# A retention and gated-MLP kernel on one core: a new written-out order of all its jobs, with other filler matmuls and other gates for transfers

## The chip, the cores and the metric

The kernel runs on one core of one Trainium2 chip. The metric is the device time of one execution in microseconds. Before the change it is 209.71 us as the median of three runs (209.13 to 210.56).

The engines of the core are named as in the profile: PE (TensorE, matmuls), PEld (PE's weight loads), DVE (VectorE), ACT (ScalarE), POOL (GpSimd) and SP (SyncE). In this kernel SP issues nearly all transfers, and it issues them in order: a transfer that waits holds every transfer behind it.

## The reference

The input is eight batches of 576 rows with eight heads of 64 columns. The first stage is a retention layer: attention without a softmax, where each score is multiplied by a power of the head's decay. The second is a gated MLP with a spatial gate, which mixes the 576 rows of a batch by the matrix w_sg.

```python
scores = scale * np.matmul(q, k.transpose(0, 1, 3, 2))
gamma = 1.0 - 2.0 ** (-5.0 - np.arange(H, dtype=np.float32))
rel = pos[:, None] - pos[None, :]
Dmat = np.where(rel >= 0, gamma[:, None, None] ** rel[None, :, :], 0.0)
x = np.matmul(scores * Dmat, v)               # heads side by side: 512 columns
...
h = gelu(x @ w_in)                            # 1024 columns
u, v = (h[..., :512], h[..., 512:])
v_n = (v - mean(v)) / np.sqrt(var(v) + 1e-06) * g_ln
v_s = np.einsum('ts,bsd->btd', w_sg, v_n) + b_sg[None, :, None]
out = x + (u * v_s) @ w_out
```

## The kernel before, in words

The eight batches are taken in four pairs. A pair has 1152 rows, or nine tiles of 128. The retention stage cuts the rows of a pair into five blocks (`RB`): four of 256 rows and one of 128 rows, which joins the end of one batch with the start of the next. So there are 20 blocks and 36 tiles. Most of the names below are those of the buffers that the profile shows.

**A block** goes through these jobs. SP loads q, k and v (`a_load`, L324 and L327; one q load may serve two blocks). POOL, and for block 0 also DVE and ACT, cast them to bf16 and multiply q and v by powers of the decay (`a_prep`, L360 and L370). PE transposes q and k (`a_T`, L407, into pp), DVE copies the transposes out (`a_Tev`, L422, qT). PE forms the scores in two halves (`a_S`, L458), DVE masks them (`a_Sev`, L471, ret). PE forms the running state k'v (`a_Z`, L494, zp), DVE adds it up and ACT casts it (`a_Zsum`, L519 and L522; `a_Zev`, L526 and L528, zb). PE forms the output in two jobs (`a_O`, `a_O2`, L540, pp), and ACT copies it out as the transposed x (`a_Oev`, L597, xT).

**A tile** then goes through these. PE forms the half of h that is normalised (`m_V`, L608, hv), ACT takes its gelu (L615, vg), DVE its mean and variance (`m_stats`, L623 and L624). POOL forms the reciprocal root (`m_rs`, L628 to L631, mv), and ACT normalises (`m_norm`, L643, vn). PE also forms the other half (`m_U`, L655, hu), and ACT takes its gelu (L665, uT).

**A batch**, once its five tiles are normalised, goes through the spatial gate: eight jobs of five matmuls against the transposed w_sg (`m_W`, L674, wp), whose results DVE multiplies into uT (L684). These are called the gating matmuls in the text. Then come the output matmuls of each tile (`m_O`, L706, op), which ACT or DVE copies out (L725, ob), and the stores (L730). The last tile, job pair 911 and 914, is done in two halves of 256 columns.

**Once per launch**: w_in in two halves of 1 MB (jobs 3 and 9, L248) with their casts on DVE and ACT (L255, L257), w_sg in three transfers (15 and 16, L269; 17, its last 64 rows, L273) with five casts on ACT (18 to 22, L280), and w_out (job 26, L291). PE transposes w_sg in ten jobs (83, 85 to 101, `build_wT`, L793, wtp), and DVE copies each out (L797, wT). Small vectors go through `to_col` (job 75, L736) and `to_rows` (77 and 79, L758) on PE.

**The order.** There is no scheduler at run time. `Planner.add` gives every job a number, 0 to 916, in the order in which the code makes them. `ORDER` is a string of these numbers, written out in the source, and `Planner.emit` walks through it and issues each job's instructions. So an engine's order is the order of its own jobs in the string; between engines the semaphores decide. Two more kinds of words stand in the string:

```python
x, _, g = x.partition("@")
j = self.fill(x[1:]) if x[0] == "f" else self.jobs[int(x)]
...
if g:
    hold(made[0], last[g])
```

A word such as `13@77` is a gate: the first transfer of job 13 also waits for the last instruction that PE's job 77 made, and through SP's order all transfers behind it wait too. A word such as `f7w128` is a filler on PE: seven fp32 matmuls of 128 columns of zeros into a scratch tile (scr, L225) that nobody reads. Fillers stand in the string in PE's order like any other job. The old string has six fillers and eight gates.

Buffers are rings with a set number of places, which also make a job wait: eight for loads, two for qT, four PSUM banks of the kind d (hv, hu, wp, op, zp, wtp, scr) and two of the kind pp.

The jobs that the text names: 0, 1, 2 are q, k, v of block 0; 6, 7, 8 those of block 1; 13, 12, 14 k, q, v of block 2; 23, 24, 25 and 31, 32 the loads of blocks 3 and 4; 33 to 37 those of blocks 5 and 6. Job 106 is the transposes of block 0, 199 and 201 its scores, 280 and 283 hv of the first two tiles. Job 293 is the state job of block 1, 203 and 205 its scores, 284 the gelu of the second tile, 297 and 298 the output jobs of block 1. Job 328 is the first gating job, 215 and 334 are a score job of block 4 and a gating job.

Of the kernel before, what the change touches and what calls it, by code (L numbers as in the profile page):

```python
# [17 lines left out]
PR = dict(PB0=10000.0, O=4000.0, PB=9900.0, S=2000.0, S2=400.0, Z=1901.0, V=6000.0, V2=900.0, U=1260.0, W=4000.0, WS=19000.0, slack=60.0, pen=500.0)  # L18

ORDER = (  # L20
# [33 lines left out]
)  # L54


# [1031 lines left out]
```

## Time and profile before

| what | value |
|---|---|
| median of three runs | 209.71 us |
| the profiled execution, its own time | 210.52 us |
| its span in the profile | 208.8 us |
| DVE, ACT, POOL busy | 72%, 56%, 57% |
| PE weight loads busy | 66% |
| chain that ended last: PE, DMA, SP's queue, DVE, POOL | 82%, 5%, 3%, 3%, 2% |
| on that chain: gating wp, output op, hv, hu | 19%, 15%, 14%, 14% |
| on that chain: fillers scr | 2% |
| DMA | 48.36 MB, 232 GB/s in the mean |

The profile is of one execution, and times in it count from the start of the span. PE's busy time is made of modelled ends of pipelined matmuls, so a busy PE isn't PE at its peak. A row of the order of time gives the start, the length of the merged row, engine, line, operation, the tile written and the tiles read, and the count; in brackets stands how long the engine was idle before, and who ended that. A row of the chain gives the start, the length and what it was; the chain is followed back from the last instruction, at each step to what released it.

### The profile page before, as it was taken

To read this page: it belongs to the slowest core of one execution; us is meant where nothing else is said; L and a number is where in the kernel's file an instruction comes from. 1 tells how busy PE (TensorE), PEld (TensorE's weight loads), DVE (VectorE), ACT (ScalarE), POOL (GpSimd) and SP (SyncE) were. 2 spreads that over 40 slices of the span, in tenths; PEclk is the share of its full clock that TensorE was granted. 3 is DMA by queue.
4 is the path that set the end of the run, shared out by engine and by line. 5 is a ranking of instruction groups with operands and counts; after the bars stand their busy time and mean duration, and the time that the engine had idled before them with its cause. 6 is when DMAs were issued, how large, how long until landed. Compare 5 with 4: busy or idle time off the path is not lost.

```text
span 208.8 us, 7892 instructions
## 1 busy us (share of the span) xinstructions
PE 196.0 (94%) x3378; PEld 137.4 (66%) x3408; DVE 151.3 (72%) x291; ACT 116.4 (56%) x207; POOL 118.3 (57%) x169
## 2 busy tenths in 40 slices
PE   7778998899999999999999999999999999999992
PEld 6655774676666676667676777576785576476751
DVE  3587567996478598917788978897885788667573
ACT  5209487574776836478852466835635667553300
POOL 8396275987567889681980996844549134022000
PEclk9999999999999999999999999999999999999999
DMA  6999949987997995999699979996986995883825
GB/s 167 290 342 216 314 150 340 293 254 268 263 279 218 303 292 140 290 262 246 178 203 285 333 244 304 164 241 152 298 219 149 175 255 154 201 152 104 239 87 201
DMA packets 85524, 48.36 MB, mean 232 GB/s; under 512 B 36650, under 2 KB 78898, under 8 KB 85490
## 3 DMA queue, kind: packets, MB, share of 16 engines
q1 hardware_dynamic: 85472, 47.87, 88.3%
q8 instruction: 26, 0.43, 0.9%
q14 instruction: 8, 0.07, 0.1%
q10 hardware_dynamic: 18, 0.00, 0.0%
HBM read 32.79 MB, written 9.44 MB: 202 GB/s over the span
## 4 chain that ended last, share of the span: by engine, by line
PE 82%; DMA 5%; SPq 3%; DVE 3%; POOL 2%; issue 2%; DVEq 0%; POOLq 0%
PE wp L674 19%; PE op L706 15%; PE hv L608 14%; PE hu L655 14%; PE pp L540 7%; DMA ld<-in_v_dram 5%; PE pp L458 4%; PE pp L407 3%; SPq L324 3%; PE zp L494 2%; PE scr L225 2%; POOL vb L370 2%; DVE wT L797 1%; PE op L701 1%; PE wtp L793 1%
## 5 line engine op out<-in xcount | busy, mean ns | idle before, releaser
L471 DVE TENSOR_TENSOR ret<-pp,msk 128x1024 bf16<-128x1024 f32 x32 | 38.3, 1213 | 6.8 <-PE pp L458 6.8
L674 PE MATMUL wp<-wT,vn 128*128 128x288 bf16 x256 | 40.5, 286 | 0.0
L370 POOL TENSOR_TENSOR vb<-ld,gpow 128x1024 bf16<-128x1024 f32 (+1 forms) x20 | 34.5, 1731 | 10.0 <-DMA ld<-in_v_dram 7.6
L608 PE MATMUL hv<-w_in,xT 128*128 128x512 bf16 x129 | 35.7, 386 | 2.1 <-DVE wT L797 0.7
L655 PE MATMUL hu<-xT,w_in 128*128 128x256 bf16 (+1 forms) x320 | 36.5, 262 | 0.3 <-DVE w_in L255 0.3
L706 PE MATMUL op<-w_out,uT 128*128 128x512 bf16 (+1 forms) x133 | 34.3, 373 | 0.9 <-issue 0.2
L684 DVE TENSOR_TENSOR uT<-wp,uT 128x288 bf16<-128x288 f32 x64 | 27.1, 449 | 10.4 <-PE wp L674 8.9
L655 PEld LDWEIGHTS <-w_in 128*128 128x128 bf16 x320 | 28.1, 98 | 6.9 <-DVE w_in L255 0.4
L597 ACT ACTIVATE xT<-pp 128x512 bf16<-128x512 f32 (+1 forms) x40 | 20.3, 552 | 21.1 <-PE pp L540 21.1
L643 ACT ACTIVATE vn<-vg,mv 128x512 bf16<-128x512 f32 x32 | 25.4, 808 | 11.5 <-POOL mv L631 11.3
L665 ACT ACTIVATE uT<-hu 128x512 bf16<-128x512 f32 x36 | 21.0, 595 | 19.3 <-PE hu L655 19.2
L674 PEld LDWEIGHTS <-vn 128*128 128x128 bf16 x256 | 24.6, 98 | 8.4
L628 POOL TENSOR_SCALAR mv<-mv 128x2 f32<-128x2 f32 (+1 forms) x20 | 4.5, 224 | 43.7 <-DVE mv L624 37.2
L615 ACT ACTIVATE vg<-hv 128x512 f32<-128x512 f32 x36 | 21.5, 597 | 12.8 <-PE hv L608 11.8
L623 DVE BATCH_NORM_STATS2 bst<-vg 128x6 f32<-128x512 f32 x36 | 24.5, 682 | 5.0 <-ACT vg L615 5.0
L370 POOL TENSOR_TENSOR qb<-ldq,gpow 128x1024 bf16<-128x1024 f32 x14 | 26.5, 1902 | 2.4 <-DMA ldq<-in_q_dram 2.3
L725 DVE TENSOR_TENSOR ob<-op,xr 128x512 f32<-128x512 f32 (+1 forms) x28 | 18.5, 669 | 7.7 <-PE op L706 6.1
L608 PEld LDWEIGHTS <-xT 128*128 128x128 bf16 x144 | 13.4, 99 | 14.7 <-ACT xT L597 1.7
L706 PEld LDWEIGHTS <-uT 128*128 128x128 bf16 x148 | 13.6, 98 | 12.0
L674 PE MATMUL wp<-wT,vmid 128*128 128x288 bf16 x64 | 18.2, 287 | 0.0
L360 POOL CAST kb<-ld 128x1024 bf16<-128x1024 f32 x14 | 14.4, 1038 | 4.6 <-PE pp L540 2.5
L422 DVE COPY qT<-pp 128x2048 bf16<-128x2048 bf16 (+1 forms) x11 | 11.3, 1025 | 6.4 <-PE pp L407 6.4
(100 smaller groups left out, 262.2 us busy)
## 6 DMA issues: line engine op xcount, KB each, us to landing
out_dram<-ob SPq DMA_DIRECT2D x35, 256.0 KB, 2.9
ld<-in_k_dram SPq DMA_DIRECT2D x16, 512.0 KB, 5.7
ld<-in_v_dram SPq DMA_DIRECT2D x16, 512.0 KB, 6.9
ldq<-in_q_dram SPq DMA_DIRECT2D x7, 1024.0 KB, 7.6
xT<-in_moe_w_sg_dram SPq DMA_DIRECT2D x2, 576.0 KB, 5.6
ld<-in_q_dram SPq DMA_DIRECT2D x2, 512.0 KB
xT<-in_moe_w_in_dram SPq DMA_DIRECT2D x1, 1024.0 KB, 8.2
ld<-in_k_dram SPq DMA_DIRECT2D x8, 128.0 KB, 3.0
```

Source lines behind the costliest of these rows:

```text
L370: ve.tensor_tensor(dst, src, g.unsqueeze(len(src.shape) - 1).to_broadcast(list(src.shape)), op=Alu.mult)
L471: ins = nc.vector.tensor_tensor(ret[:].rearrange("p r (k t) -> p (r k) t", k=2), sc[:].rearrange("p r (k t) -> p (r k) t", k=2), (msk2 if ...
L597: nc.scalar.activation(dst, src, Act.Copy)
L608: ins = nc.tensor.matmul(hv[:], xTs[p][:, m, kk, :], w_in[:, kk, F2:], start=(kk == 0), stop=(kk == KK - 1))
L615: unfence(nc.scalar.activation(vgs[i][:], cur.pop(("hv", i))[:], Act.Gelu_apprx_tanh), ("V", i))
L623: nc.vector.bn_stats(bst[:], vgs[i][:])
L643: nc.scalar.activation(vn[:], vg[:], Act.Identity, scale=mv[:, s, 2:3], bias=mv[:, s, 3:4])
L655: ins = nc.tensor.matmul(hu[:, n, :], w_in[:, kk, 128 * c:128 * c + 128], xTs[p][:, m:m + w, kk, :], start=(kk == 0), stop=(kk == KK - 1), ...
L665: unfence(nc.scalar.activation(uTs[p][:, c0:c1, 128 * m:128 * m + 128 * w], cur.pop(("hu", i, half))[:], Act.Gelu_apprx_tanh), ("U", i, half))
L674: ins = nc.tensor.matmul(ps[:], vns[t0 + j][e][:, 128 * c:128 * c + 128], wT[e][j][:, half * HS:(half + 1) * HS], start=(j == 0), stop=(j ...
L684: ins = nc.vector.tensor_tensor(uTs[p][:, c, col:col + HS], cur.pop(("wp", b, c, half))[:], uTs[p][:, c, col:col + HS], op=Alu.mult)
L706: ins = nc.tensor.matmul(op[:], uTs[p][:, c, r], w_out[:, c, cs], start=(p >= XP and c == 0), stop=(c == KK - 1), skip_group_check=True)
```

## The change

`ORDER` is replaced by another string of the same 917 jobs; no other line of the kernel differs. It changes the order of every engine, SP among them.

The fillers: the old ones are f2w64, f1w128, f5w64, f4w192, f7w128, f3w256. The new ones are f2w64, f1w256, f1w64, f7w256, f6w256, f2w192, f1w128, f3w192, f1w64, f1w192. All of the new ones stand before block 1's first output job, as all of the old ones do.

The gates: the old ones are 13@77, 9@297, 33@215, 36@361, 48@151, 55@461, 508@489, 745@798. The new ones are 7@75, 9@298, 33@215, 36@334, 44@219, 349@450, 53@481, 55@491, 583@241, nine in all.

PE's jobs up to the first weight transposes, with `to_col` (75) behind the transposes of block 0 instead of before them:

```
before: f2w64 f1w128 f5w64 75 f4w192 106 199 201 77 271 276 277 79 111 280 205 293 f7w128 203 283 116 f3w256 207 297 298 83 101 85
after:  f2w64 f1w256 f1w64 f7w256 106 75 f6w256 199 77 201 271 f2w192 276 277 111 f1w128 280 203 293 205 283 f3w192 116 f1w64 f1w192 79 207 297 83 99 298 89
```

SP's first transfers:

```
before: 1 0 6 2 7 3 8 13@77 12 17 16 15 14 23 9@297 24 31 25 32 34 33@215 26 36@361 35
after:  17 0 1 2 6 7@75 3 8 13 12 15 16 14 23 9@298 24 31 25 32 26 33@215 36@334 34 35
```

ACT's casts of w_sg, in the old list 22 21 20, then the gelu 284, then 19 18; in the new one 22 is ACT's first job, and 284 18 295 19 20 21 follow one another. On DVE the evacuation of block 3's q (123) stood ahead of the statistics 306 and now stands behind them. At the end DVE emptied the two halves of the last tile as 915 912 and now empties them as 912 915; their stores follow the same order.

The diff, cut to the parts of which the text speaks:

```diff
 ORDER = (
-    '1 0 103 f2w64 6 f1w128 f5w64 2 7 75 f4w192 76 104 3 8 106 107 199 200 201 202 108 105 74 109 73 77 13@77 271 '
-    '273 12 276 17 277 278 5 79 279 111 78 72 272 274 4 112 80 16 280 110 113 114 15 14 81 281 205 293 23 f7w128 206 '
-    '203 283 116 282 294 296 204 117 f3w256 207 275 295 22 21 20 284 19 18 297 9@297 298 82 299 115 285 208 24 83 31 '
-    '101 85 317 318 290 25 32 118 119 84 102 320 300 291 319 292 97 89 86 90 98 91 95 321 87 322 92 96 93 301 304 '
-    '122 94 323 88 302 11 305 10 303 123 306 326 120 124 34 286 309 99 100 314 316 287 310 311 126 121 307 127 315 '
...
-    '893 898 901 894 899 895 908 902 903 909 910 904 905 906 911 914 915 912 916 913 '
+    '17 0 22 f2w64 1 103 72 2 6 104 f1w256 f1w64 105 73 108 f7w256 106 75 107 76 7@75 109 3 f6w256 8 13 199 200 12 '
+    '77 201 202 271 f2w192 273 276 277 110 113 114 78 272 111 f1w128 274 4 112 278 5 15 16 280 279 275 14 203 23 293 '
+    '205 283 204 281 282 294 81 284 18 295 19 20 21 206 296 285 f3w192 116 f1w64 f1w192 79 117 207 208 80 297 83 74 '
+    '290 115 99 84 100 298 9@298 89 90 91 24 95 31 101 102 92 317 25 93 94 96 318 85 86 97 98 314 315 87 32 118 119 '
+    '291 292 320 300 319 299 82 321 322 316 323 326 11 120 124 88 10 304 301 302 122 305 303 306 123 26 286 309 288 '
...
+    '887 891 896 888 897 889 893 898 901 894 899 895 902 903 904 905 906 908 909 910 911 914 912 915 913 916 '
 )
```

54 rows, old and new, of the table ORDER are left out of this document.

## The prediction

> **What bounds the kernel now.** I read the page's busy shares first, then two stretches in the windows view (columns: length, busy time and instructions of PE, PEld, DVE, ACT, POOL, then clock, DMA share, GB/s).
>
> ```profile
> span 208.8 us, 7892 instructions
> PE 196.0 (94%) x3378; PEld 137.4 (66%) x3408; DVE 151.3 (72%) x291; ACT 116.4 (56%) x207; POOL 118.3 (57%) x169
> 0.00:45.00 45.00, 38.22 (x663) 29.30 (x669) 30.96 (x72) 26.11 (x43) 30.67 (x56) 1.00 0.96 258
> 45.00:205.00 160.00, 157.74 (x2721) 108.11 (x2748) 119.61 (x219) 90.29 (x164) 87.68 (x114) 1.00 0.88 225
> ```
>
> From 45 us on PE is busy 157.74 of 160 us. The lists hold the same real PE jobs, so behind 45 us a new order can save at most those 2.3 us. In front of it PE issues a fifth of its instructions in 45 us: the ramp. So I take the chain that ended last, in order of time, up to the first gating matmul (start, length, what):
>
> ```profile
> 8.38 9.96 DMA ld<-in_v_dram
> 18.48 1.91 POOL vb L370
> 20.43 0.64 PE zp L494 x27
> 21.07 3.28 PE scr L225 x14
> 24.35 0.57 PE pp L458 x14
> 24.92 0.42 PE hv L608
> 25.39 0.59 PE hv L608 x2
> 25.99 0.34 PE pp L407 x16
> 26.33 1.49 PE scr L225 x6
> 28.07 0.56 PE pp L540 x40
> 29.06 0.94 PE wtp L793 x15
> ...
> 37.52 1.11 DVE qT L422
> 38.63 0.61 DVE bst L623
> 41.42 1.87 POOL vb L370
> 43.34 0.44 PE zp L494 x32
> 45.63 0.47 PE wp L674 x3
> ```
>
> The chain runs through fillers (scr, L225), matmuls that compute nothing: f7w128 (each fp32 filler is recorded as two matmuls, so x14) for 3.28 us and f3w256 (x6) for 1.49 us, 4.77 us together. They don't fill a wait, they are one: the score job behind f7w128 (203) has the inputs of its twin 205, which stands ahead of the filler in the list. Why so long? PE's order of time:
>
> ```profile
> 1.24 3.67 PE L225 MATMUL scr<-warm 128*128 128x64 f32 x16 [1.24 <-DVE warm L183]
> 6.06 2.93 PE L225 MATMUL scr<-warm 128*128 128x192 f32 x8
> 8.92 1.04 PE L407 MATMUL pp<-ident,qb 64*128 64x64 bf16 x32
> 11.28 1.07 PE L458 MATMUL pp<-qT 64*64 64x128 bf16 x32 [1.32 <-DVE qT L422]
> 16.38 1.04 PE L407 MATMUL pp<-ident,qb 64*128 64x64 bf16 x32
> 17.63 0.59 PE L608 MATMUL hv<-w_in,xT 128*128 128x512 bf16 x1 [0.22 <-DVE w_in L255]
> 56.20 0.64 PE L407 MATMUL pp<-ident,qb 64*128 64x64 bf16 x32
> 60.43 0.42 PE L494 MATMUL zp<-vb,kb 64*64 64x64 bf16 x32
> ```
>
> The same 32 transposes take 1.04 us at 8.92 and 16.38 but 0.64 at 56.20; 27 state matmuls take 0.64 us at 20.43, 32 take 0.42 at 60.43. A filler of 128 columns took 3.28/14 = 0.234 us in the run from 21.07, one of 256 columns 1.49/6 = 0.248 us from 26.33: 1.83 against 0.97 ns a column. PE ran at about half rate until some 25 us, though the clock column says 1.00 throughout. It changed after the one unbroken stretch of work before then, 21.07 to 25.9, 4.9 us. The busy stretch of 6.06 to 9.96, 3.9 us with the transposes, did not change it.
>
> The Trainium skill (TensorE: Matmul & The Clock Gate, Part 1) says that the array starts at half clock and is let go after a busy window of about 3.4 us; the halving agrees, and 4.9 us against 3.9 us fits a window that does not start with the work. By its remark that this ramp costs under 1% of a span, the whole change could give at most 2.1 us; the 3.28 us row alone is larger, so I let the row decide.
>
> **The change, part by part.**
>
> *First fillers.* Before the first transposes (job 106) PE now gets f2w64, f1w256, f1w64, f7w256: 6 matmuls of 64 columns (3.67/16 = 0.23 us) and 16 of 256. At half rate 256 columns are not in the trace: 2.93/8 = 0.366 us for 192 gives 0.49 us, as an estimate. All slow: 1.24 + 1.4 + 7.8 = 10.4 us; with the change of rate after 4.9 us: 7 at 0.49, 9 at 0.25, ending at 8.3. The transposes' inputs were there by 8.92, and come up to 0.5 later now, since 144 KB of w_sg (job 17) are issued ahead of q and k (290 GB/s, row below). So they start at 8.3 to 10.4 instead of 8.92. f6w256 then stands ahead of the first scores: 12 x 0.25 = 3.0 us in a wait of 1.3, so scores at about 12.6 instead of 11.28 (5.9 us and 17.5 if slow: 10.4 + 1.04 + 0.2 + 5.9). Cover: the first hv needs w_in, which ended its wait at 17.63. f2w192, f1w128: under 1.2 us together, in front of the same wait. I count all at nothing; without the cover 1.3 us.
>
> *Fillers on the chain.* Between the state job at 20.43 and the second block's output job stand now f3w192, f1w64, f1w192. Fast: 8 x 0.19 + 2 x 0.19 = 1.9 us; slow: 8 x 0.366 + 2 x 0.23 = 3.4. Against 4.77: -2.9 or -1.4. I take -2.9, because by then PE has had its unbroken 4.9 us twice over.
>
> *Real jobs at full rate.* On the chain zp, 14 scores and hv: 0.64 to 0.42, 0.57 to 0.40, and hv by a quarter of its 1.01: -0.6.
>
> *The gate 7@75.* SP's first five loads are 144 KB and four of 512 KB, 2.2 MB.
>
> ```profile
> 5.00:10.00 5.00, 4.07 (x41) 3.48 (x41) 2.65 (x11) 1.36 (x3) 1.59 (x3) 1.00 1.20 290
> 17.00:19.00 2.00, 1.56 (x19) 0.69 (x14) 2.00 (x3) 1.95 (x4) 0.53 (x1) 1.00 1.00 147
> 27.50:30.20 2.70, 2.58 (x101) 1.97 (x99) 1.75 (x5) 2.17 (x4) 2.37 (x6) 1.00 0.10 35
> 28.68 0.37 SPq L248 DMA_DIRECT2D uT<-in_moe_w_in_dram  x1
> ```
>
> At 290 GB/s they end near 10. Job 7 (block 1's k), behind it w_in's half, v, and all later loads, wait in SP's queue until job 75 has run behind the transposes, 8.8 to 10.6. A gated load's data moves 1.5 us after its issue (28.68, 30.2), so DMA idles 0.3 to 2.1 us. Against that, the old gate 13@77, whose slow stretch is 17 to 19 (147 GB/s), is gone: some 1 us. For v of block 1, the chain's head, -1 to +2.1; I take +0.6.
>
> *The w_sg casts.* They must end before the ten weight transposes (wtp).
>
> ```profile
> 18.12 1.03 SPq L269 DMA_DIRECT2D xT<-in_moe_w_sg_dram  x2
> xT<-in_moe_w_sg_dram SPq DMA_DIRECT2D x2, 576.0 KB, 5.6
> 23.41 1.24 ACT L280 ACTIVATE wnat<-xT 128x576 bf16<-128x576 f32 x2
> 26.08 0.60 ACT L615 ACTIVATE vg<-hv 128x512 f32<-128x512 f32 x1 [1.44 <-PE hv L608]
> 26.58 1.25 ACT L280 ACTIVATE wnat<-xT 128x576 bf16<-128x576 f32 x2
> ```
>
> Two stood behind vg, which waited for the late hv. In the new list vg (284) and all four follow one another, so they end 1.3 us behind the last w_sg data (19.15 + 5.6 = 24.8, an estimate, +0.6): 26.7, against wtp at 29.06: -2.4 there, where the sum above gives -2.9. For wtp the tighter one holds.
>
> *To the first gating matmul.* DVE empties the ten wtp tiles and does the statistics between 29.5 and 39.45. The new list puts the q evacuation (1.11) behind the last of them: -1.1 on DVE, -3.5 with the shift. But POOL's mv job stands behind two k casts, whose loads follow gate 9@298, two wtp later than 9@297 (+0.6): -2.9 + 0.6 = -2.3. POOL, then, sets it: the last vb, the state job and wp come 2.3 us earlier.
>
> *Rest.* Other gates (36@334, 44@219, 349@450, 53@481, 55@491, 583@241) hold SP with loads or stores behind them. Their cover is POOL's spare time: beyond 46 us it waited for q as below and idled mostly for DVE's statistics.
>
> ```profile
> POOL mv L628 <- DVE mv L624: 35.0, 13, 6.2
> POOL qb L370 <- DMA ldq<-in_q_dram: 2.3, 2, 2.0
> ```
>
> The tightest is 36@334, which also holds job 34 (block 5's k): one more 512 KB load, 1.8 us, at the k transposes. I take 0; without cover +1, and by the 2.3 us of PE's idle time the rest may go 1 either way. At the tail DVE empties the halves in PE's order:
>
> ```profile
> 204.98 0.76 DVE L725 TENSOR_TENSOR ob<-op,xr 128x256 f32<-128x256 f32 x2 [0.18 <-PE op L706]
> ```
>
> The 0.18 us goes: -0.2.
>
> **Sum**: -2.9 (fillers) -0.6 (rate) +0.6 (gate 7@75) +0.6 (gate 9@298) -0.2 (tail) = -2.5. The span goes from 208.8 to 206.3, the profiled execution from 210.52 to 208.0; the median of the runs stands 0.81 below it (209.71), so 207.2. Bounds: the best head (-1.6 against my value) and 1 in the rest give -5.1, 204.6; I end at 205.0, since the w_sg casts would then hold wtp. The slow price of the chain's fillers (+1.5), the worst head (+1.5) and 1 in the rest give +1.5, 211.2; I end at 210.4, since these don't all come together.
>
> **Rivals.**
> 1. *The transfers take it back.* v of block 1 and w_sg land 2.1 us later by the idle of 7@75, nothing returned for 13@77. For: 96% DMA share in the ramp. Against: the 2.7 us of idle DMA at 27.5 show that the load behind isn't bound by volume. Sum with +2.1: -1.0, so 208.7.
> 2. *Slower: the wide fillers run at half rate.* If PE's rate does not change until past 25 us, or falls back in a pause, the scores start at 17.5 instead of 11.28, 6.2 later; of these I let 1.1 lie in the first hv's wait for w_in, so it starts at 22.7 instead of 17.63. Then come hv (1.8), a score, a state and a score job (0.3, 0.6, 0.3) and the second hv at 25.8 instead of 24.92, since f7w128 (3.28) is gone; behind it 1.1 of hv, 3.4 of fillers, 0.4 of transposes and 0.9 of small jobs: the output job at 31.6 instead of 28.07, +3.5, 213.2. It decides from the point where the 7-filler run, 4.9 us in, has not changed the rate. For it: the stretch of 3.9 us that did nothing. Against: this run is unbroken and twice as long.
> 3. *More.* DVE's shorter stretch counts and 9@298 costs nothing, since volume doesn't bind the k loads: -2.9 - 1.1 - 0.2 = -4.2, 205.5. For: DVE is in the chain from 37.52 to 39.45. Against: the k loads behind 9@298.
> 4. *The list only moves the waits.* PE's dense part catches the old line: k transposes behind 36@334, a gating run without its vn. The -2.3 are lost again, the tail's -0.2 stays: 209.5. For it: PE is on the chain nearly throughout. Against: DVE and POOL, at 72% and 57%, are seldom the last to end there.
>
> The Trainium skill (TensorE: Matmul & The Clock Gate, Part 4) holds that transposes do not count as PE work for the clock. The stretch of 6.06 to 9.96 agrees: without its transposes it is 2.9 us. No filler run here contains transposes, so no number changes by it.
>
> **Chances.** Forecast (-1.5 to -3.5) 0.48, more (3) 0.14, transfers (1) 0.15, moved waits (4) 0.12, slower (2) 0.11. One per cent, 2.1 us, is about what a measurement of this kernel can tell from no change (its runs span 209.13 to 210.56). Faster by over 1% means below 207.6: 0.7 of the forecast, which reaches from 206.2 to 208.2, and all of rival 3, 0.48. Slower is rival 2, 0.11. The rest, 0.41, lies between.
>
> **What would show it.** Right: 32 transposes near 9 us take about 0.64 us; fillers of 256 columns take 0.25 us from some 8 us on; second block's hv near 22, wtp near 27, first wp near 42 to 43.5; PE as dense behind it. Wrong: 0.49 us for late fillers (2); a DMA stretch near 10 to 12 us without bytes and v's cast beyond 20.5 (1); PE idle by more than 3.3 us behind its first wp (4).

## The result, and the profile after

The kernel after takes 211.88 us (median of 20 runs, 210.28 to 214.20), the kernel before, measured beside it, 210.13 us (20 runs). The ratio is 1.0081, 95% interval 1.0055 to 1.0107: about 1.7 us longer. Executions more than 1.5% above the fastest of their kernel, three of these 20 among them, count as slow and stand in no ratio and in no mean of spans below. The forecast was 207.2 us with a range up to 210.4; the time lies above it.

The profiled execution of the kernel after takes 210.98 us, its span is 209.3 us. First the page: span, busy shares, the granted clock in 40 slices, and the shares of the chain that ended last.

```profile
span 209.3 us, 7914 instructions
PE 196.5 (94%) x3414; PEld 135.9 (65%) x3414; DVE 150.3 (72%) x291; ACT 116.3 (56%) x207; POOL 118.2 (56%) x169
PEclk9999699999999999999999999999999999999999
PE 70%; DMA 12%; POOL 9%; issue 3%; ACT 2%; SPq 1%; DVE 1%; DVEq 0%; POOLq 0%; ACTq 0%
```

Two things are new. In the fifth slice, 21 to 26 us, the granted clock dips to 0.6. And on the chain DMA and POOL have 21% together, where they had 7% before: the chain runs through transfers and POOL's casts more often, though PE is busy 94% in both. PE's order of time in the front shows where:

```profile
1.24 6.50 PE L225 MATMUL scr<-warm 128*128 128x64 f32 x22 [1.24 <-DVE warm L183]
8.73 0.64 PE L407 MATMUL pp<-ident,qb 64*128 64x64 bf16 x32 [1.00 <-ACT qb L358]
9.46 2.86 PE L225 MATMUL scr<-warm 128*128 128x256 f32 x12
12.24 0.42 PE L458 MATMUL pp<-qT 64*64 64x128 bf16 x16
...
17.55 1.03 PE L608 MATMUL hv<-w_in,xT 128*128 128x512 bf16 x4
...
22.09 0.45 PE L494 MATMUL zp<-vb,qb 64*64 64x64 bf16 x32 [2.78 <-POOL vb L370]
...
22.69 1.89 PE L608 MATMUL hv<-w_in,xT 128*128 128x512 bf16 x4
24.37 1.97 PE L225 MATMUL scr<-warm 128*128 128x192 f32 x6
...
26.61 0.82 PE L225 MATMUL scr<-warm 128*128 128x64 f32 x4
...
28.54 0.73 PE L793 MATMUL wtp<-ident,wnat 128*128 128x128 bf16 x10
```

Up to the first hv everything came as forecast. The 22 first filler matmuls end at 7.74 us, the transposes take 0.64 us, a filler of 256 columns 2.86/12 = 0.24 us, and the first hv runs at full rate (1.03 us, four matmuls). Then PE waits 2.78 us for block 1's v. Behind that wait the same four hv matmuls take 1.89 us, and the fillers of 192 columns 1.97/6 = 0.33 us instead of 0.19: PE is back at half rate. The first wtp starts at 28.54 us (forecast 26.7; 28.99 in PE's order of time of before, 29.06 on its chain).

The wait goes back to the gate. SP's issues, the chain's next pieces, POOL's order of time and the windows view:

```profile
9.56 0.37 SPq L324 DMA_DIRECT2D ld<-in_k_dram  x1
...
10.60 0.51 SPq L324 DMA_DIRECT2D ld<-in_v_dram  x1
```

```profile
10.60 9.47 DMA ld<-in_v_dram
...
20.14 1.91 POOL vb L370
...
22.09 0.45 PE zp L494 x32
```

```profile
9.40:11.30 1.90, 1.90 (x10) 1.67 (x11) 1.78 (x5) 0.00 (x0) 1.75 (x1) 1.00 0.73 172
19.00:22.00 3.00, 0.32 (x12) 0.17 (x12) 2.01 (x3) 2.72 (x5) 1.86 (x1) 1.00 0.86 200
22.00:25.50 3.50, 3.41 (x56) 2.40 (x56) 2.14 (x4) 0.88 (x2) 2.78 (x5) 0.59 1.09 289
```

7@75 holds SP until 9.56. The transfers fall to 172 GB/s, and v lands at 10.60 + 9.47 = 20.07 us, where before it landed at 8.38 + 9.96 = 18.34: 1.73 us late. PE is busy for 0.32 us between 19 and 22 us. From 22 us on the granted clock is 0.59 in the mean. By the clock's record in the trace the rate is at half from 22.6 to 26.1 us, 3.4 us.

Later, in the chain, then POOL's order of time here and in the profile of before:

```profile
31.99 1.64 ACT xT L597 x4
```

```profile
42.06 3.76 POOL L370 TENSOR_TENSOR vb<-ld,gpow 128x1024 bf16<-128x1024 f32 x2
```

```profile
41.38 3.76 POOL L370 TENSOR_TENSOR vb<-ld,gpow 128x1024 bf16<-128x1024 f32 x2
```

The last two vb casts before the gating run start at 42.06 us, 0.7 later than in that profile, where the forecast had them 2.3 earlier. At the end DVE is done sooner behind PE, as forecast:

```profile
204.21 1.35 DVE L725 TENSOR_TENSOR ob<-op,xr 128x512 f32<-128x512 f32 x3 [0.17 <-PE op L706]
```

DVE ends at 204.21 + 1.35 = 205.56, before at 204.98 + 0.76 = 205.74. But from there to the end of the span it is 3.7 us, before 3.1.

### The profile page after: what moved, and what is told of

It is laid out like the page before. It is cut to its first block, busy times and chain, and to the rows that moved or that the text cites. A ratio compares the mean times of both kernels' runs of the same rounds, so it can differ in the third digit from the quotient of the medians.

```text
span 209.3 us, 7914 instructions
## 1 busy us (share of the span) xinstructions
PE 196.5 (94%) x3414; PEld 135.9 (65%) x3414; DVE 150.3 (72%) x291; ACT 116.3 (56%) x207; POOL 118.2 (56%) x169
## 4 chain that ended last, share of the span: by engine, by line
PE 70%; DMA 12%; POOL 9%; issue 3%; ACT 2%; SPq 1%; DVE 1%; DVEq 0%; POOLq 0%; ACTq 0%
PE wp L674 17%; PE op L706 13%; PE hv L608 12%; PE hu L655 12%; PE pp L540 7%; DMA ld<-in_v_dram 5%; POOL vb L370 4%; DMA ldq<-in_q_dram 4%; PE pp L458 3%; DMA ld<-in_k_dram 3%; PE pp L407 2%; PE zp L494 2%; POOL qb L370 1%; PE scr L225 1%; POOL mv L629 1%
## 5 line engine op out<-in xcount | busy, mean ns | idle before, releaser
L370 POOL TENSOR_TENSOR vb<-ld,gpow 128x1024 bf16<-128x1024 f32 (+1 forms) x20 | 34.5, 1731 | 12.6 <-DMA ld<-in_v_dram 12.5
L608 PE MATMUL hv<-w_in,xT 128*128 128x512 bf16 x144 | 36.5, 386 | 0.5 <-ACT vg L615 0.5
L655 PE MATMUL hu<-xT,w_in 128*128 128x256 bf16 (+1 forms) x320 | 35.7, 262 | 0.3 <-DVE w_in L255 0.3
L706 PE MATMUL op<-w_out,uT 128*128 128x512 bf16 (+1 forms) x148 | 35.4, 374 | 0.0
L643 ACT ACTIVATE vn<-vg,mv 128x512 bf16<-128x512 f32 x32 | 24.9, 807 | 12.6 <-POOL mv L631 12.6
L370 POOL TENSOR_TENSOR qb<-ldq,gpow 128x1024 bf16<-128x1024 f32 x14 | 26.4, 1902 | 9.7 <-DMA ldq<-in_q_dram 9.6
L665 ACT ACTIVATE uT<-hu 128x512 bf16<-128x512 f32 x36 | 20.5, 591 | 13.6 <-PE hu L655 13.4
L597 ACT ACTIVATE xT<-pp 128x512 bf16<-128x512 f32 (+1 forms) x40 | 20.1, 557 | 14.3 <-PE pp L540 14.3
L725 DVE TENSOR_TENSOR ob<-op,xr 128x512 f32<-128x512 f32 (+1 forms) x28 | 18.0, 665 | 5.5 <-PE op L706 5.5
L629 POOL TENSOR_TENSOR mv<-mv,mhalf 128x2 f32<-128x2 f32 (+1 forms) x20 | 14.1, 707 | 1.7
```

Source lines behind the costliest of these rows:

```text
L370: ve.tensor_tensor(dst, src, g.unsqueeze(len(src.shape) - 1).to_broadcast(list(src.shape)), op=Alu.mult)
L597: nc.scalar.activation(dst, src, Act.Copy)
L608: ins = nc.tensor.matmul(hv[:], xTs[p][:, m, kk, :], w_in[:, kk, F2:], start=(kk == 0), stop=(kk == KK - 1))
L643: nc.scalar.activation(vn[:], vg[:], Act.Identity, scale=mv[:, s, 2:3], bias=mv[:, s, 3:4])
L655: ins = nc.tensor.matmul(hu[:, n, :], w_in[:, kk, 128 * c:128 * c + 128], xTs[p][:, m:m + w, kk, :], start=(kk == 0), stop=(kk == KK - 1), ...
L665: unfence(nc.scalar.activation(uTs[p][:, c0:c1, 128 * m:128 * m + 128 * w], cur.pop(("hu", i, half))[:], Act.Gelu_apprx_tanh), ("U", i, half))
```

## The experiments

All were run beside the kernel before, 12 times each, gate_old 6 times; a ratio is to that kernel's runs on the same chip. The intervals reach 0.003 to 0.004 to each side, so two ratios can differ by chance by nearly 0.005 (an estimate from them). "Dips" counts the executions whose mean granted clock lies below 0.995; 3.4 us at half rate give 0.992, as in the profile of the kernel after. The clock's record starts with its first change, so a late rise doesn't show in it, and dips are compared among kernels with the new first fillers only. A mean clock doesn't say where in the execution the dip lies. The two spans are the means of the executions with and without a dip.

| kernel | ratio, 95% interval | dips | spans with, without |
|---|---|---|---|
| after | 1.0081, 1.0055 to 1.0107 | 16 of 20 | 209.64, 208.72 |
| before_again | 1.0004, 0.9970 to 1.0038 | | |
| free7 | 1.0030, 0.9997 to 1.0064 | 7 of 12 | 208.66, 208.02 |
| fillpause | 1.0027, 1.0000 to 1.0054 | 0 of 12 | -, 208.73 |
| actorder | 1.0071, 1.0039 to 1.0102 | 8 of 12 | 209.44, 209.10 |
| free7_g297 | 0.9993, 0.9956 to 1.0029 | 6 of 12 | 208.43, 207.52 |
| mended | 0.9941, 0.9914 to 0.9968 | 0 of 12 | -, 207.12 |
| mended_again | 0.9968, 0.9933 to 1.0004 | 0 of 12 | -, 207.50 |
| mended_nof | 0.9987, 0.9954 to 1.0020 | 6 of 12 | 208.40, 206.85 |
| mended_nochain | 0.9989, 0.9955 to 1.0023 | 3 of 12 | 208.40, 207.51 |
| wide_old | 1.0016, 0.9982 to 1.0051 | 12 of 12 | 208.79, - |
| wide_lean | 1.0093, 1.0059 to 1.0127 | 12 of 12 | 210.38, - |
| hold_old | 1.0011, 0.9970 to 1.0051 | 3 of 12 | 209.85, 208.14 |
| hold_lean | 1.0006, 0.9970 to 1.0042 | 10 of 12 | 208.64, 207.10 |
| gate_old | 1.0161, 1.0121 to 1.0202 | | |
| front_new | 0.9989, 0.9955 to 1.0023 | | |
| front_old | 1.0084, 1.0050 to 1.0119 | | |

My theory after the result: gate 7@75 makes v late, PE's pause lets the rate fall, and both together eat the gain. Rivals: the fillers never were on the path (then the -2.9 is wrong in itself); the loss lies in ACT's order, in the gate on 9, or behind 46 us.

### How much of the old time was the late rise: before_again

No edit.

> The kernel of before, unchanged, for the spans and granted clocks of more executions: the pages shown so far have one. If the time of the new list hangs on PE's clock falling back in a pause, these executions should show a clock of 1.00 nearly always and spans of 208 to 209.5 us; if the clock falls here as often as in the new list (mean 0.990), the fall can't be the difference. Ratio 1.00.

PE's order of time in this profile, whose span is 206.7 us:

```profile
20.73 1.83 PE L225 MATMUL scr<-warm 128*128 128x128 f32 x14
...
24.15 1.56 PE L225 MATMUL scr<-warm 128*128 128x256 f32 x6
...
26.88 1.01 PE L793 MATMUL wtp<-ident,wnat 128*128 128x128 bf16 x15
```

Here f7w128 takes 1.83 us instead of 3.28, since by the clock's record the rate rose at 18.9 us and not at 25.1. The first wtp starts at 26.88 instead of 28.99 us, and the span is 2.1 us shorter. So my 4.77 us of fillers were the price in one execution with a late rise; in this one they are 3.39. The expectation of a clock of 1.00 nearly always was wrong: 4 of the 12 executions have 0.974 to 0.984. Their mean span is that of the other eight (208.03 and 208.06), so in the old list a low mean clock goes with no longer span. None of the four was profiled; in gate_old, with the old fillers, such a stretch lies from 13 to 26.5 us. That the fall of the rate costs time in the new list rests on the next experiments, not on this one.

### The gate and the pause: free7, fillpause, gate_old

```diff
-... 107 76 7@75 109 3 f6w256 ...
+... 107 76 7 109 3 f6w256 ...
```

> The new list without its first gate: the word 7@75 becomes 7, so block 1's k, w_in's half and block 1's v are issued behind q without waiting for PE. Theory A (the late v sets the ramp, and the pause that it makes lets the clock fall): DMA no longer idles near 10 to 11 us, v's cast starts near 18.8 instead of 20.14, the pause ahead of the second state job shrinks from 2.8 to about 1.4 us, the clock holds at 1.00, the second hv takes 1.0 instead of 1.9 us, the weight transposes start near 26.5 instead of 28.5, and the span falls by 1.5 to 2 us. Rival theory B (the ramp is set by ACT's new order and by later waits): v comes earlier, but the span falls by under 0.5 us.

```diff
-... 203 23 293 205 ...
+... 203 23 f5w256 293 205 ...
```

> The new list with one filler more, f5w256 (about 2.5 us at full rate), put into PE's pause ahead of the second state job; no transfer is moved. Theory A1 (of the late v it is the fall of the clock that costs, not the waiting): v's cast still starts at about 20.1, but the clock stays at 1.00, the second hv takes 1.0 instead of 1.9 us, the three fillers behind it 1.9 instead of 3.1, and the span falls by 0.8 to 2 us. Rival A2 (the late arrival itself costs): the clock holds and the span stays within 0.4 us.

Without the gate the ratio falls from 1.0081 to 1.0030. PE's order of time in free7 (two lines more in its source: L227 is L225 of the others, L496 L494, L795 L793):

```profile
21.14 0.45 PE L496 MATMUL zp<-vb,qb 64*64 64x64 bf16 x32 [1.85 <-POOL vb L372]
...
22.61 1.14 PE L227 MATMUL scr<-warm 128*128 128x192 f32 x6
...
25.95 0.55 PE L795 MATMUL wtp<-ident,wnat 128*128 128x128 bf16 x3
```

The wait is 1.85 us, the rate stays up in this execution, the fillers take the 1.14 us (0.19 each) that I had forecast, and wtp starts 2.6 us earlier than in the kernel after. With the gate left in and a filler in the pause there is no dip (0 of 12). PE's order of time in fillpause (lines as in free7):

```profile
22.78 0.45 PE L496 MATMUL zp<-vb,qb 64*64 64x64 bf16 x32 [0.88 <-POOL vb L372]
...
27.60 1.05 PE L795 MATMUL wtp<-ident,wnat 128*128 128x128 bf16 x10
```

From the state job to wtp it is 4.82 us here and 4.81 in free7, but 6.45 in the kernel after (22.09 to 28.54). So of the 2.6 us at wtp between the kernel after and free7 the half rate makes 1.6, and the earlier start of the state job (21.14 instead of 22.09) makes 1.0. In the time each edit alone gives about 0.005, 1.1 us: clear of chance, if barely for free7, and less than the 1.5 to 2 us that I expected of the gate. Neither alone beats the kernel before. Nor does free7 where the rate held: its five executions without a dip have a mean span of 208.02 us, the twelve of before_again 208.05.

The gate alone, in the old list:

```diff
-... f5w64 2 7 75 f4w192 76 104 3 8 106 107 ...
+... f5w64 2 75 f4w192 76 104 106 7@106 3 8 107 ...
```

> The kernel before with a gate on job 7 behind block 0's transposes (7@106), as 7@75 in the new list, and nothing else moved but the words it needs. Theory (the gate leaves the transfers idle and makes block 1's v late, here and in the new list): block 1's v lands 1 to 2 us later than 18.3, the state job 293 starts near 20.5 to 21.5 instead of 19.2 to 19.8, the time is 0.8 to 1.8 us longer, ratio 1.004 to 1.009. Rival (the idle stretch at 13@77 shrinks by as much, as the prediction's bound of -1 has it): ratio 0.998 to 1.002.

The windows view and PE's order of time:

```profile
8.50:11.50 3.00, 1.68 (x54) 1.14 (x56) 2.32 (x9) 0.00 (x0) 2.77 (x2) 1.00 0.48 116
13.00:26.50 13.50, 10.14 (x147) 7.15 (x150) 8.09 (x15) 7.82 (x14) 7.77 (x10) 0.50 0.96 265
```

```profile
22.59 0.65 PE L494 MATMUL zp<-vb,qb 64*64 64x64 bf16 x32 [2.41 <-POOL vb L370]
23.16 3.35 PE L225 MATMUL scr<-warm 128*128 128x128 f32 x14
...
26.91 1.04 PE L608 MATMUL hv<-w_in,xT 128*128 128x512 bf16 x4
```

It costs 3.4 us (0.0161, six runs), about twice the upper end of what I expected. The idle transfers (116 GB/s) delay v, PE waits 2.41 us for it, and the state job starts at 22.59 us, in the profile of before at 20.43. The rate doesn't fall in that wait: it had risen early and is at half from 13 us on, so f7w128 runs at half rate as in the profile of before. So this profile shows the price of the late v, and not that of a fall behind it. The rival, that 13@77's idle stretch pays for it, falls.

### The other orders of the front: actorder, free7_g297

```diff
-... 291 292 320 300 319 299 82 ...
+... 299 300 291 292 320 319 82 ...
```

> The new list with one change in ACT's order: the two copies of block 1's output (299, 300) stand ahead of the normalisations and of block 2's copies (291, 292, 320, 319), as 299 does in the old list, instead of behind 320. Theory B (ACT's order delays the way to the first gating matmul): ACT's idle 2.5 us at 29.5 to 32 goes, the first normalised tiles come 0.7 to 1.1 us earlier, POOL's mv at 40.5 starts near 39.5, and the span falls by about 0.7. Theory A alone: the clock still falls, and the span stays within 0.3 us.

The ratio is 1.0071, within chance of the kernel after: the difference of 0.001 is uncertain by some 0.004 either way, so ACT's order alone doesn't make the 0.008.

```diff
-... 76 7@75 109 ...
+... 76 7 109 ...
-... 298 9@298 89 ...
+... 298 9@297 89 ...
```

> The new list without the gate on 7, and with 9@297 instead of 9@298. The prediction's term for 9@298 (+0.6, two weight transposes later): 0.6 to 1.0 us below free7, ratio 0.998 to 1.000. Rival (the gate has cover, and what mended gained over free7 came from the filler in front of 293 and from ACT's order): as free7, ratio 1.002 to 1.004.

0.9993 against 1.0030 for free7: 0.0037, of the size that the theory gave, but the intervals overlap. And the two profiles agree to 0.1 us in PE's starts from the state job of block 1 to that of block 4 (first wtp 25.95 and 25.86, block 4's state job 42.49 and 42.54 us), where my term had placed the delay. So the mechanism that I gave for the +0.6 (k's loads late, POOL's mv late) isn't seen; what the gate on 9 costs stays open.

### A version that beats both: mended, mended_again, mended_nof, mended_nochain

```diff
-... 107 76 7@75 109 ...
+... 107 76 7 109 ...
-... 203 23 293 205 ...
+... 203 23 f3w256 293 205 ...
-... 298 9@298 89 ...
+... 298 9@297 89 ...
-... 291 292 320 300 319 299 82 ...
+... 299 300 291 292 320 319 82 ...
-... 914 912 915 913 916
+... 914 915 912 916 913
```

> The new list with five of its parts undone: 7 without its gate, 9@297 instead of 9@298, f3w256 in front of 293, ACT's 299 300 ahead of 320, and the old order of the last two evacuations. Theory (gate 7@75 with the fall of the rate, then 9@298 and ACT's order, then the tail, are what the new list gives away): near 2.5 us below the kernel after and 0.7 us below the kernel before, ratio 0.993 to 0.999. Rival (what is lost lies in the order behind 46 us, about 0.7 us): ratio 1.000 to 1.003, as free7 and fillpause had it.

> mended once more, on the chip of this call. Theory: 0.992 to 0.996, the rate up in every execution. Rival (its gain was of that chip): 0.998 to 1.002.

208.93 us (12 runs) against 210.33 of the kernel before, and on a second chip 209.43 against 210.06. The first interval lies wholly below 1, the second touches it, and 0.9968 lies between what the theory and the rival of mended_again had. No execution has a dip. PE's order of time in mended, around the filler:

```profile
19.27 1.56 PE L225 MATMUL scr<-warm 128*128 128x256 f32 x6
21.23 0.45 PE L494 MATMUL zp<-vb,qb 64*64 64x64 bf16 x32 [0.40 <-POOL vb L370]
```

The filler lies wholly in the wait for v. Taken out again:

```diff
-... 203 23 f3w256 293 205 ...
+... 203 23 293 205 ...
```

> mended without f3w256 in front of 293 (so free7_g297 with ACT's order and the old tail). Theory (the filler holds the rate, which falls without it in about half of the executions at 1.3 to 1.7 us each): the rate falls in some executions, ratio 0.997 to 1.000. Rival (ACT's order and the tail brought it): as mended, 0.993 to 0.996, and no difference with the rate.

```profile
21.55 0.44 PE L494 MATMUL zp<-vb,qb 64*64 64x64 bf16 x32 [2.23 <-POOL vb L370]
...
23.43 2.13 PE L225 MATMUL scr<-warm 128*128 128x192 f32 x6
```

A wait of 2.23 us was enough here for the rate to fall. 6 of 12 executions have a dip, and their span is some 1.5 us longer than that of the other six (208.40 and 206.85), which are as short as mended. So the filler's worth is that the rate holds; the ratios by themselves (0.9987 and, on the same chip, 0.9968) are too near to each other to show it.

```diff
-... 285 f3w192 116 f1w64 f1w192 79 ...
+... 285 116 79 ...
```

> mended without f3w192, f1w64 and f1w192 (1.1 + 0.8 us at full rate between the second tile's hv and block 1's output job). The prediction's first term (fillers there cost their length): 1.5 to 1.9 us below mended, ratio 0.985 to 0.988. Rival (w_sg's casts end at 26.5 us and hold wtp, so these fillers lie in a wait): as mended, 0.992 to 0.996, or above it if the rate falls in the pause.

By the prediction's first term this had to gain 1.9 us. It gained nothing: 0.9989, and without a dip its span is that of mended_again on the same chip (207.51 and 207.50). PE waits instead:

```profile
23.11 0.41 PE L407 MATMUL pp<-ident,qb 64*128 64x64 bf16 x16 [0.47 <-DVE ret L471]
...
24.89 0.32 PE L458 MATMUL pp<-qT 64*64 64x64 bf16 x16 [1.00 <-DVE qT L422]
```

The score job behind the transposes needs their evacuation, some 1 us on DVE; the fillers stood in that time. From the state job to the first wtp it is 4.82 us with the fillers (21.23 to 26.05 in mended) and 4.82 without (21.00 to 25.82).

### The fillers in the old list: wide_old, wide_lean, hold_old, hold_lean

```diff
-1 0 103 f2w64 6 f1w128 f5w64 2 7 75 f4w192 76 104 3 8 106 107 ...
+1 0 103 f2w64 6 f1w256 f1w64 2 7 f7w256 104 3 8 106 75 107 76 ...
```

> The kernel before with the new list's first fillers alone (one of 256, one of 64 and seven of 256 columns in front of job 106, and job 75 behind 106); the long f7w128 and f3w256 stay. Theory (the early full rate is the useful part of the change, and the old kernel's time hangs on when its rate rises, at 18.9 us in one profile and at 25.1 us in another): the clock rises near 5.6 us, f7w128 takes 1.6 instead of 3.28 us, the span is near 206.5 in every execution against a mean of 208.1 before, ratio 0.992 to 0.996. Rival (the front is bound by block 1's v, 18.3 us, and w_in, 17.4 us, whatever the rate): ratio 0.998 to 1.002.

wide_lean is this without f7w128 and f3w256.

> As wide_old, and f7w128 and f3w256 are left out as well. The prediction's main step (a filler on the chain costs its length, -2.9): 1.6 + 1.5 us less than wide_old, a span near 203.5, ratio 0.978 to 0.984. Rival (behind the state job of block 1 the loads and w_sg's casts set the pace, so the fillers fill waits once the rate is full): at most 1 us below wide_old, 0.988 to 0.996. Second rival (without them PE pauses, the rate falls for a window of 3.4 us): equal to or above wide_old.

Windows of wide_old and, below, of wide_lean:

```profile
12.00:16.00 4.00, 2.35 (x77) 1.59 (x77) 3.80 (x10) 0.38 (x1) 3.72 (x7) 0.85 1.11 344
16.00:18.00 2.00, 1.98 (x40) 1.42 (x39) 1.74 (x4) 1.89 (x3) 0.94 (x2) 0.50 1.17 161
```

```profile
20.00:24.00 4.00, 3.17 (x66) 1.61 (x67) 3.72 (x6) 2.55 (x6) 2.38 (x3) 0.50 0.96 306
```

The early rise was not kept, and wide_old is as the rival had it (1.0016): the clock fell again near 15 us, where the old list has only short work in front of the first hv (PE busy 2.35 of 4 us). Without the two long fillers it stayed at half until past 24 us, and the time is 0.9% above the kernel before. Leaving out matmuls that compute nothing made the kernel longer. Why is open: in the profiles the half rate isn't where the time goes. wide_lean is ahead of wide_old up to the first gating matmul (44.48 and 44.90 us) and falls behind at 49 us, in a stop of PE for nothing that the profile shows:

```profile
48.89 0.30 PE L540 MATMUL pp<-qT,zb 64*64 64x128 bf16 x6 [1.06 <-issue]
```

hold_old adds what holds the rate:

```diff
-... 75 107 76 199 ...     ... 276 17 277 ...          ... 16 280 ...
+... 75 107 76 f6w256 199 ...     ... f2w192 276 17 277 ...   ... 16 f1w128 280 ...
```

> wide_old with the new list's next fillers as well: f6w256 in front of 199, f2w192 in front of 276, f1w128 in front of 280; everything else is the old list. Theory (in wide_old the rate rose early and fell again at 15 us, because PE then had only short work in front of the first hv; the fillers in the waits hold it, and f7w128 and f3w256 cost 1.6 and 1.5 us at full rate, mostly in waits): the rate stays up, the span is 206.0 to 206.7 in nearly every execution, ratio 0.989 to 0.995. Rival (the rate of the first 20 us does not matter, since block 1's v and w_sg bound the front): ratio 0.998 to 1.002, as wide_old had it.

hold_lean then moves f3w256 into the wait for v, and leaves f7w128 out:

```diff
-... 281 205 293 23 f7w128 206 203 ... 117 f3w256 207 ...
+... 281 205 f3w256 293 23 206 203 ... 117 207 ...
```

> hold_old without f7w128 and f3w256 on the chain, and with f3w256 in front of 293, in the wait for block 1's v, so that the rate has no pause to fall in. The prediction's first term taken alone: 1.8 + 1.6 us less on the chain at full rate, some 3 us below hold_old, ratio 0.985 to 0.990. Rival (w_sg's casts, then the statistics and block 2's v set the pace, so what PE no longer does it waits for): the first wtp starts 1 us earlier (26.1) and the time is 0 to 0.8 us below hold_old, ratio 0.996 to 1.001.

In hold_old 9 of 12 executions have no dip, yet the ratio is 1.0011: my theory of the early rise falls for the old list. PE's order of time in hold_lean, then in wide_lean, around the first wtp:

```profile
24.12 0.32 PE L458 MATMUL pp<-qT 64*64 64x64 bf16 x16 [1.09 <-DVE qT L422]
...
25.91 0.69 PE L540 MATMUL pp<-ret,vb 64*64 64x128 bf16 x19 [1.14 <-issue]
...
27.07 1.78 PE L793 MATMUL wtp<-ident,wnat 128*128 128x128 bf16 x15
```

```profile
27.16 1.53 PE L793 MATMUL wtp<-ident,wnat 128*128 128x128 bf16 x15 [0.84 <-ACT wnat L280]
```

With the fillers off the chain, block 1's output job starts 1.8 us earlier (24.27 us, in hold_old 26.03), but the first wtp doesn't: 27.07 against 27.12. PE waits 1.09 us for DVE's evacuation, 1.14 us for nothing that the profile shows, and in wide_lean for w_sg's cast. The ratio is 1.0006, no gain. One reservation: 10 of 12 executions of hold_lean have a dip. The two without have a span of 207.10 us, hold_old's without 208.14; two are too few to tell, and it would still be less than half of the 3.4 us by which the chain was relieved.

### Behind 46 us: front_new, front_old

front_new is mended up to job 334 with all other jobs in the old list's order; front_old is the old list up to job 361 with the others in the new order.

> mended up to the job ahead of 334 (some 43 us), then all other jobs in the old list's order, with the old gates. Theory (behind 45 us the new list is some 0.6 us less dense than the old, and some 0.4 us longer between PE's last matmul and the end of the span): 0.6 to 1.0 us below mended, a span near 206.2, ratio 0.988 to 0.992. Rival (the part behind 45 us is worth the same in both): as mended, 0.993 to 0.995.

> The old list up to job 361 (some 48 us), then all other jobs in the new list's order, with the new gates. Theory: 0.6 to 1.0 us above before, ratio 1.003 to 1.005. Rival (the part behind is worth the same in both, or better in the new list): 0.998 to 1.001.

Windows from 45 to 204 us in front_old, then in before_again (the sums over five windows):

```profile
sum 159.00, PE 156.42 PEld 106.77 DVE 117.01 ACT 88.80 POOL 87.44; mean PE 31.28 PEld 21.35 DVE 23.40 ACT 17.76 POOL 17.49
```

```profile
sum 159.00, PE 157.35 PEld 106.37 DVE 118.26 ACT 89.12 POOL 86.56; mean PE 31.47 PEld 21.27 DVE 23.65 ACT 17.82 POOL 17.31
```

The new order behind the old front costs 0.8%, more than the 0.3 to 0.5% of the theory, and PE has 0.9 us less work in this stretch. But the old order behind the new front, from which I expected a gain, is none over mended (0.9989 against 0.9941 and 0.9968); in its profile PE is idle for 1.06 of the 5 us behind the seam (43 to 48 us), in mended for 0.26. So each order behind 46 us may fit its own front alone, and what the new one costs by itself can't be read from the two. It may well be part of the 1.7 us; that stays open.

## Why the prediction was wrong, point by point

**First fillers: right.** Block 0's transposes take 0.64 us, a filler of 256 columns 0.24, the first hv runs at full rate, the scores start at 12.24 us (12.6 forecast). The rate rose at 5.6 us, 4.3 us after the first filler; in the profile of before it rose at 25.1 us, 4.0 us into the stretch that I had taken for 4.9 us.

**Fillers on the chain, -2.9: the step that failed.** I subtracted 1.9 from 4.77 us, because the fillers "don't fill a wait, they are one". Two things were wrong. The 4.77 us were read off one execution, in which f7w128 ran at half rate because the rate rose at 25.1 us; in before_again, with a rise at 18.9 us, the same two fillers took 3.39 us. The Trainium skill (TensorE: Matmul & The Clock Gate, Part 1) says that the clock's window runs freely, so that the cold stretch at a kernel's start differs from run to run; the two profiles of one kernel agree. And a filler's length was not what leaving it out gives back: it gained nothing that could be measured (mended_nochain 0.9989 beside mended_again 0.9968, hold_lean 1.0006 beside hold_old 1.0011), since PE waits for DVE's evacuation, for w_sg's casts or in a stop that the profile doesn't explain. At wtp the new list without the gate stands 0.9 us ahead of before_again (25.95 and 26.88), not 2.4. From the state job to the first wtp it takes 4.81 us, before_again 6.52; as mended_nochain takes 4.82 without any filler there, the shorter fillers alone don't explain this, and what shortened it stays open. I had held the 3.28 us row against the remark of the Trainium skill (TensorE: Matmul & The Clock Gate, Part 1) that the ramp costs under 1% of a span, and let the row decide; the row was one draw.

**Real jobs at full rate, -0.6: of the other sign.** The state job took 0.45 us as forecast, but the second hv 1.89 instead of the 1.01 that I had read for before, since the rate had fallen: 0.9 lost, 0.2 gained.

**Gate 7@75, +0.6: mis-sized.** v came 1.73 us later, near the upper bound of +2.1. The gate makes about 1.0 of it: without it, in free7, POOL's cast of v still starts at 19.18 us (20.14 in the kernel after, 18.48 before), so the rest lies in the new order of the loads. Taking the gate out is worth 0.005, 1.1 us. What I left out of this step is what followed: in 16 of 20 executions of this kernel the rate dipped, in the profiled one right behind the wait of 2.78 us. Rival 2 has the words "falls back in a pause", but I had tied it to the first fillers and priced it at 213.2; rival 1 has the late v without the rate. What happened in the profile is the two in a row.

**Gate 9@298, +0.6: open**, as told above.

**w_sg casts, and the way to the first gating matmul, -2.3 there: failed too.** The casts ended at 26.5 us in mended, near the 26.7 I gave; in the kernel after at 27.8, behind a gelu that waited for the hv at half rate. But the gain at wtp doesn't reach the last vb casts. ACT's and POOL's order of time in free7 (L599 is L597 of the others, L372 L370), then POOL's in before_again:

```profile
30.12 1.64 ACT L599 ACTIVATE xT<-pp 128x256 bf16<-128x256 f32 x4 [1.92 <-PE pp L542]
...
40.19 3.76 POOL L372 TENSOR_TENSOR vb<-ld,gpow 128x1024 bf16<-128x1024 f32 x2
```

```profile
39.27 3.77 POOL L370 TENSOR_TENSOR vb<-ld,gpow 128x1024 bf16<-128x1024 f32 x2
```

Even without the gate and with the rate up they start 0.9 us later than in before_again, though wtp started 0.9 us earlier. From the first wtp to these casts it is 14.2 us in free7 and 14.4 in free7_g297, 12.4 in both profiles of the old list. I had not costed that ACT's 299 and 300 stand behind 320: ACT copies block 1's output out at 30.12 us (31.99 in the kernel after), in before_again from 27.40 us on, and the gelu, DVE's statistics and POOL's mv stand behind. With 299 and 300 moved forward it is 13.2 us in mended and 13.3 in mended_again. In the time this doesn't show: actorder differs by 0.001 from the kernel after, and mended_nof, which differs from free7_g297 by this and the tail, has 0.9987 against 0.9993.

**The tail, -0.2: right in DVE, and lost behind it.** DVE ended 0.18 us earlier, the span 0.5 later. mended has the old order of the halves and nearly the same long end (3.5 us from DVE's last result), so the order of the halves isn't the cause.

**The chances.** Slower by over 1% had 0.11, no change 0.41; the time is 0.8% longer, in the band "within 1%" but beyond my upper bound. The sum of my worst terms, with the chain's fillers at half rate, gave 211.2, and I ended at 210.4 because "these don't all come together"; the measured time lies above both. They aren't independent: in the profile the late v stands ahead of the half rate. That the time lies in the band of no change is no merit of the forecast: the band was made of small gains, late transfers and moved waits, and what filled it was a gain that wasn't there and a loss that I had priced too low.

## What to carry to other kernels

A filler on the chain is not yet a cost: ask what PE would wait for without it, and whether the rate would fall in that wait; only then subtract. Costs that hang on the clock need more than one execution of the kernel before. A gate on the queue that issues all loads delays every load behind it, and where PE waits on one of these, the pause can cost a second time through the rate; a filler in just that pause, which nothing waits for, held the rate here (0 dips in 12 executions with it, 6 without, on one chip).

## What the runs showed of the hardware that I had not expected

- The rate fell after waits of 2.78 us (after) and 2.23 us (mended_nof) with short work beside them, and held through 1.85 us in the profile of free7 and 2.00 us in that of free7_g297; other executions of these two kernels have a dip (7 and 6 of 12). The Trainium skill (TensorE: Matmul & The Clock Gate, Part 1) gives an idle window of about 3.4 us for the fall. The half-rate stretch lasted about as long as such a window (3.4 us in the profile of the kernel after), but the waits that brought it were shorter.
- Two executions of the kernel before differ by 2.1 us in span (208.8 and 206.7) with the first wtp 2.1 us apart, and the rest alike.
- Between DVE's last result and the end of the span lie 3.1 us in the profiles with the old list's last part and 3.5 to 3.8 in those with the new one's (after, free7, actorder, mended, mended_again). Which of the last instructions stands still there I can't show; the cause is open.
